# Second MLP's weight units: cast, low part and stores at other places in a pair of steps

## The chip, the cores and the metric

The kernel runs on one core of a Trainium2 chip. The metric is the device time of one execution in microseconds; of several runs the median is taken. Engines are named as the profile names them: PE (TensorE), DVE (VectorE), ACT (ScalarE), POOL (GpSimd) and SP (SyncE), whose queue, SPq, issues nearly all transfers.

## The reference

Three layers follow one another over 2304 tokens (4 batches of 576) of width 512:

```
attention, per batch and head (8 heads of 64):
    scores = (q @ k.T) / sqrt(64)
    out    = (scores * D) @ v          D[i, j] = gamma_h ** (i - j) for i >= j, else 0
first MLP:    h = max(x @ w_in, 0);   y = (h * h) @ w_out        512 -> 2048 -> 512
second MLP:   h = x @ w_in;  g = h * clip(h + 3, 0, 6) / 6;  y = g @ w_out
```

All inputs and the output are float32.

## The kernel before

**Precision.** PE multiplies in a shortened float32 (fp32r). Each operand is therefore held as a high part (its value cast) and a low part (the value less its high part), and a product is three matmuls: high by high, low by high, high by low.

**First stage.** The attention is computed as a recurrence over 18 chunks of 128 tokens and feeds the first MLP directly. The tokens of the first MLP go in five blocks of 512, 384, 512, 384 and 512 columns (`BLOCKS`, blocks 0 to 4), each in 16 steps over the 2048 inner columns: 80 steps, counted by `i` in the main loop. In step `i` the program writes, in this order: unit work of slot 0; `h_part` of step `i + 1` (12 matmuls at L514, then ACT's relu at L523, DVE's product at L525, ACT's high part of g at L527); unit work of slot 1; DVE's low part of g (L533); a piece of the attention for a later block (`retention`); and `a_part` of step `i` (12 matmuls at L551 that need g of this step). Each engine works its own list in the order written, and waits at an instruction until what it needs is there. PE's order in a step is therefore h of the next step, the piece of attention, a of this step.

**Retention.** In most even steps of blocks 1 to 3 a chunk has either its scores and states (L399, L410; DVE L418, L435, L437; then loads of the next chunk's k and q, L235, L236) or its values (L447, L457; ACT L468 and DVE L469 take the output into x; then loads of v, L243, and four small loads of qs, L383).

**Units.** The second MLP multiplies with seven products of combined blocks in place of eight, so its weights are combined once, in DRAM, while the first stage runs: 32 units, one begun every two steps from step 14 on. With `i - 14 = 2n + odd`, `unit_work` hands unit `n` and the units behind it to:

- `unit_load` (L596): two loads of raw words into `raw`, one buffer;
- `unit_scale` (L602, L603, ACT): scales the words;
- `unit_narrow` (L610, L611, DVE): joins them to float32 in a tile `seven`, of which there are two;
- `unit_combine` (four DVE operations, L618 to L621 or L623 to L626);
- `unit_cast` (L631, ACT): the high parts into `uhi`, tag "high", one buffer;
- `unit_low` (L636, DVE): the low parts, in place in `seven`;
- `unit_store` (L643 for the in-weights, L645 for the out-weights): 448 KB of high parts (`x` = 0) or low parts (`x` = 1) to DRAM.

A tile whose buffer was stored from is written again only when that store has landed. In step 72 (`half`) the loads of the second MLP's x (L691) are written behind the step's retention, and in the steps behind it DVE and ACT make x's operands (L695, L698, L702). Then the last units' work, the eviction of block 4 and the second MLP follow, in which PE runs L1025 and L1079.

Of the kernel before, what the change touches and what calls it, by code (L numbers as in the profile page):

```python
# [25 lines left out]
NF = DFF // P  # L26
# [58 lines left out]
def retention_moe_kernel(ctx: ExitStack, tc, qk, kv, w1, w2, cst, out):  # L85
# [144 lines left out]
    def load_qk(c):  # L230

        if c < NCHUNK:
            t = apool.tile([P, 2, NPAIR, P], F32, tag="q", name=f"q_{c}")
            k = apool.tile([P, DM], F32, tag="k", name=f"k_{c}")
            nc.sync.dma_start(k, kv[c, :, 0])  # L235
            nc.sync.dma_start(t, qk[c].rearrange("p x (n t) -> p x n t", n=NPAIR))  # L236
            ch[c] = [t[:, 0], t[:, 1], k]
# [147 lines left out]
    def scale_q(c):  # L385
        eng(c).tensor_tensor(qs[c], qs[c], since, ALU.mult)  # L386

    def scale_k(c):
        k3 = ch[c][2].rearrange("p (h d) -> p h d", h=H)
        eng(c).tensor_tensor(k3, k3, kd.unsqueeze(2).to_broadcast([P, H, D]), ALU.mult)  # L390

    def scores(c):
        q, kt, k, v = ch[c]
        _, straddle, ends = where(c)
        at = sums[c] = ps_at.tile([P, 2, 512], F32, tag="at", name=f"sc_{c}")
        for n in range(NPAIR):
            for e in range(2):
                for i in range(2):
                    nc.tensor.matmul(  # L399
                        at[hb(i), e, BT * n : BT * n + BT],  # L400
                        kt[hb(e), n, hb(i)],
                        q[hb(e), n, hb(i)],
                        start=True,
                        stop=True,
                    )

        for n in range(NPAIR):
            for i in range(1 if straddle else 0, 1 if ends else 2):
                for e in range(2):
                    nc.tensor.matmul(  # L410
                        at[hb(e), i, 256 + D * n : 256 + D * n + D],
                        k[hb(i), cols(n, e)],
                        v[hb(i), cols(n, e)],
                        start=True,
                        stop=True,
                    )
        t = probs[c] = apool.tile([P, 2, NPAIR * BT], F32, tag="p", name=f"p_{c}")
        nc.vector.tensor_tensor(t, at[:, :, :256], decay, ALU.mult)  # L418

    def age_state(c):  # L420
        new_state(c + 1)
        fresh, straddle, _ = where(c)
        if fresh or straddle:
            return
        m3, b3 = (t.rearrange("p (h d) -> p h d", h=H) for t in (middle(c), before(c)))
        nc.vector.tensor_tensor(m3, b3, gh[:BT].unsqueeze(2).to_broadcast([BT, H, D]), ALU.mult)

    def sum_states(c):
        fresh, straddle, ends = where(c)
        for i in range(1 if straddle else 0, 1 if ends else 2):  # L430
            for e in range(2):
                u = sums[c][hb(e), i, 256:].rearrange("p (n d) -> p n d", n=NPAIR)
                o = heads((before(c + 1) if i else middle(c)), e)
                if (fresh, straddle)[i]:
                    nc.vector.tensor_copy(o, u)  # L435
                else:
                    nc.vector.tensor_tensor(o, u, heads(middle(c), e), ALU.add)  # L437

    def values(c):
        v = ch[c][3]  # L440
        fresh, straddle, _ = where(c)
        at = os_[c] = ps_at.tile([P, 2, 512], F32, tag="at", name=f"o_{c}")
        read = [i for i in range(2) if not (fresh, straddle)[i]]
        for n in range(NPAIR):
            for i in range(2):
                for e in range(2):
                    nc.tensor.matmul(  # L447
                        at[hb(e), i, BT * n : BT * n + BT],
                        v[hb(i), cols(n, e)],
                        probs[c][hb(i), e, BT * n : BT * n + BT],  # L450
                        start=n == 0,
                        stop=n == NPAIR - 1 and i not in read,
                    )
        for n in range(NPAIR):
            for i in read:
                for e in range(2):
                    nc.tensor.matmul(  # L457
                        at[hb(e), i, BT * n : BT * n + BT],
                        rec[c][hb(i), cols(n, e)],
                        qs[c][hb(i), block(n, e)],  # L460
                        start=False,
                        stop=n == NPAIR - 1,
                    )

    def into_x(c, xt, off):
        x4 = xt[:, :, :, off : off + P].rearrange("p x n (i t) -> p x n i t", i=2)
        o = os_[c][:, :, :256].rearrange("p i (n t) -> p n i t", n=NPAIR)
        nc.scalar.activation(x4[:, 0], o, AF.Copy)  # L468
        nc.vector.tensor_tensor(x4[:, 1], o, x4[:, 0].bitcast(F32), ALU.subtract)  # L469
# [5 lines left out]
    def retention(i):  # L475
        for c, s in enumerate(SCORES, n0):
            if i == s - 1:
                scale_k(c)
                age_state(c)
            elif i == s:  # L480
                scores(c)
                if c < 7:
                    scale_q(c)
                else:
                    sum_states(c)
                load_qk(c + 1)
            elif i == s + 1:
                if c < 7:
                    sum_states(c)
                else:  # L490
                    scale_q(c)
            elif i == s + 2:
                blk = next(b for b in range(nblk) if start[b + 1] > c * P)
                values(c)
                into_x(c, xs[0, blk], c * P - start[blk])
                load_v(c + 1)
# [150 lines left out]
    def unit_work(i, slot):  # L647

        n, odd = divmod(i, 2)

        def on(lag, fn, *a):
            if 0 <= n - lag < 4 * NJ:
                fn(n - lag, *a)

        if slot == 0 and not odd:
            on(1, unit_narrow)
            on(0, unit_load)
            on(2, unit_store, 0)
        elif slot == 0:
            on(2, unit_low)  # L660
            on(2, unit_store, 1)
        elif not odd:
            on(1, unit_combine)
        else:
            on(0, unit_scale)
            on(1, unit_cast)


    x_ops = {}
# [156 lines left out]
    def first_between(f):  # L826
        if f + 2 < NF:
            cast_w(0, f + 2, (0,))
            low_w(0, f + 2, (0,))

    for i, (ph, blk, f) in enumerate(steps):
        if blk == 0:
            if 0 < f:
                low_w(0, f, (1,), nc.vector)
            if f == 0:
                first_sum(n0 - 1)
            if f + 3 < NF:
                scale_w(0, f + 3, (0,))
            if f + 2 < NF:
                scale_w(0, f + 2, (1,))  # L840
                narrow_w(0, f + 2, (0,))
            if f + 1 < NF:
                narrow_w(0, f + 1, (1,))
        unit_work(i - NF + 2, 0)
        if i + 1 < len(steps):
            h_part(*steps[i + 1], lambda: first_between(f) if blk == 0 else None)
            if blk == 0 and f + 1 < NF:
                cast_w(0, f + 1, (1,))
        if blk == 0:
            if f + 4 < NF:  # L850
                load_w(0, f + 4)
        if f < NF - 1:
            unit_work(i - NF + 2, 1)
        if i + 1 < len(steps) and blk:
            g_low(*steps[i + 1])
        if blk + 1 < nblk:
            if f == 0:
                new_x(0, blk + 1)
        retention(i)
        if blk == 0:  # L860
            g_low(*steps[i + 1])
        if i == half:

            right.close()
            p1a = xpre = pool(ctx, "p1a", 1, side="right")
            x_tiles(p1a)
            x_first = x_stages(0)
            for st in x_first:
                do(st[0])
        if half < i <= half + RING - 1:  # L870
            ring_load(i - half - 1)
        if i > half:
            k = i - half
            if k < len(x_first[0]):
                for st in x_first:
                    do(st[k])
        a_part(ph, blk, f)
        if f == NF - 1 and blk + 1 < nblk:
            evict(blk)
            unit_work(i - NF + 2, 1)  # L880
# [1 line left out]

    unit_work(len(steps) - NF + 1, 1)
    for v in range(len(steps) - NF + 2, len(steps) - NF + 4):
        unit_work(v, 0)
        unit_work(v, 1)
    left.close()
    p1c = pool(ctx, "p1c", 1, side="left")
    held = [
# [242 lines left out]
```

## Time and profile before

| | |
|---|---|
| median of 3 runs | 826.24 us (826.21 to 828.54) |
| the profiled execution | 825.94 us, its span 824.1 us |
| PE busy | 805.2 us (98%) |
| DVE busy | 597.0 us (72%) |
| ACT busy | 391.9 us (48%) |
| POOL busy | 164.1 us (20%) |
| SP's DMA queue | 188.40 MB, 72.6% of 16 engines |
| mean granted clock of PE | 0.998 of 2.4 GHz |
| mean of one, ACT | relu L523 0.55 us, g L527 0.59, x L468 0.58, cast L631 0.94 |
| mean of one, DVE | product L525 0.63 us, g's low part L533 0.68, unit's low part L636 1.08 |
| the four x loads of step 72 (L691) | issued from 429.79 on, the last at 432.09 |
| a pair of steps of block 2 (512 columns), with retention | 12.2 us between L551 groups at 211.80 and 224.00 |

Busy time tells how much an engine worked, not whether anyone waited for it. A wait in the profile is put down to the work that came last before the engine went on. Times of the trace are counted from the span's start. The first stage takes about 468 us of the span, the second MLP six stretches of 58.2 us on PE, and the tail 6.5 us.

### The profile page before, as it was taken

To read this page: it belongs to the slowest core of one execution; us is meant where nothing else is said; L and a number is where in the kernel's file an instruction comes from. 1 tells how busy PE (TensorE), PEld (TensorE's weight loads), DVE (VectorE), ACT (ScalarE), POOL (GpSimd) and SP (SyncE) were. 2 spreads that over 40 slices of the span, in tenths; PEclk is the share of its full clock that TensorE was granted. 3 is DMA by queue.
4 is the path that set the end of the run, shared out by engine and by line. 5 is a ranking of instruction groups with operands and counts; after the bars stand their busy time and mean duration, and the time that the engine had idled before them with its cause. 6 is when DMAs were issued, how large, how long until landed. Compare 5 with 4: busy or idle time off the path is not lost.

```text
span 824.1 us, 15603 instructions
## 1 busy us (share of the span) xinstructions
PE 805.2 (98%) x5876; PEld 744.6 (90%) x5876; DVE 597.0 (72%) x1098; ACT 391.9 (48%) x724; POOL 164.1 (20%) x146
## 2 busy tenths in 40 slices
PE   8999999988999999989999999999999999999996
PEld 7788889987888889989888899999999999999996
DVE  5888887566765576667546877988677987678764
ACT  1887744333433444334445433566234655334552
POOL 3312230111011001100000055600155400355300
PEclk9999999999999999999999999999999999999999
DMA  8876625666666466657447797889987979987785
GB/s 330 303 250 216 219 68 167 186 191 187 216 196 206 144 199 195 200 167 219 148 136 252 225 351 251 294 308 277 273 273 241 344 260 289 274 261 262 259 258 109
DMA packets 181899, 189.59 MB, mean 230 GB/s; under 512 B 60608, under 2 KB 135488, under 8 KB 181824
## 3 DMA queue, kind: packets, MB, share of 16 engines
q1 hardware_dynamic: 180224, 188.40, 72.6%
q8 instruction: 46, 0.75, 0.4%
q10 hardware_dynamic: 1600, 0.20, 0.2%
q14 instruction: 29, 0.24, 0.1%
HBM read 149.76 MB, written 38.80 MB: 229 GB/s over the span
## 4 chain that ended last, share of the span: by engine, by line
PE 83%; DVE 7%; DMA 5%; ACT 2%; issue 2%; SPq 1%; POOL 0%; DVEq 0%
PE z L1025 21%; PE z L1079 21%; PE acc L551 19%; PE h L514 18%; DMA w_in_hl<-seven 3%; DMA w_out_hl<-seven 1%; DMA kv<-kv_dram 1%; DVE r L525 1%; DVE seven L636 1%; DVE seven L611 1%; PE o L447 1%; SPq L383 1%; PE sc L399 1%; DVE state L437 1%; PE o L457 1%
## 5 line engine op out<-in xcount | busy, mean ns | idle before, releaser
L551 PE MATMUL acc<-g,w 128*128 128x512 f32 (+1 forms) x960 | 215.0, 372 | 4.9 <-ACT g L527 4.4
L514 PE MATMUL h<-x,w 128*128 128x512 f32 (+2 forms) x972 | 210.9, 365 | 1.6 <-ACT w L165 0.9
L551 PEld LDWEIGHTS acc<-g,w 128*128 128x128 f32 x960 | 172.9, 188 | 31.6 <-ACT g L527 6.8
L514 PEld LDWEIGHTS h<-x,w 128*128 128x128 f32 x972 | 175.8, 188 | 24.4 <-ACT w L165 1.6
L1025 PE MATMUL z<-xop,ring 128*128 128x384 f32 x1008 | 175.2, 334 | 0.0
L1079 PE MATMUL z<-spl,ring 128*128 128x384 f32 x1008 | 175.2, 334 | 0.0
L1025 PEld LDWEIGHTS z<-xop,ring 128*128 128x128 f32 x1008 | 174.8, 188 | 0.1
L1079 PEld LDWEIGHTS z<-spl,ring 128*128 128x128 f32 x1008 | 174.8, 188 | 0.0
L947 POOL TENSOR_TENSOR aop<-aop,aop 128x384 f32<-128x384 f32 x96 | 107.7, 1133 | 301.5 <-DVE aop L944 180.6
L961 DVE TENSOR_TENSOR spl<-aop,spl 128x384 fp32r<-128x384 f32 x168 | 97.8, 608 | 22.3 <-ACT spl L957 21.4
L957 ACT ACTIVATE spl<-aop 128x384 fp32r<-128x384 f32 x168 | 85.9, 523 | 55.3 <-PE z L1079 52.3
L527 ACT ACTIVATE g<-r 128x512 fp32r<-128x512 f32 (+1 forms) x80 | 47.1, 589 | 112.4 <-DVE r L525 112.4
L941 ACT ACTIVATE aop<-held,con 128x384 f32<-128x384 f32 x72 | 44.4, 617 | 108.1 <-DVE held L907 107.5
L523 ACT ACTIVATE r<-h 128x512 f32<-128x512 f32 (+1 forms) x80 | 44.2, 552 | 108.3 <-PE h L514 107.0
L525 DVE TENSOR_TENSOR r<-r,h 128x512 f32<-128x512 f32 (+1 forms) x80 | 50.5, 631 | 54.5 <-ACT r L523 53.9
L907 DVE TENSOR_TENSOR held<-z,held 128x384 f32<-128x384 f32 x120 | 66.5, 554 | 26.7 <-PE z L1025 24.4
L533 DVE TENSOR_TENSOR g<-r,g 128x512 fp32r<-128x512 f32 (+1 forms) x80 | 54.5, 681 | 22.2 <-ACT g L527 22.0
L944 DVE SCALAR_TENSOR_TENSOR aop<-aop,held 128x384 f32<-128x384 f32 x72 | 49.8, 692 | 17.8 <-ACT aop L941 16.1
L610 DVE TENSOR_SCALAR seven<-uraw 128x512 int32<-128x512 int32 x32 | 13.8, 432 | 40.1 <-DMA w_in_hl<-seven 18.3
L386 POOL TENSOR_TENSOR qs<-qs,con 128x512 f32<-128x512 f32 x11 | 14.7, 1336 | 121.1 <-DMA qs<-qk_dram 84.6
L172 POOL TENSOR_TENSOR w<-wt,w 128x512 fp32r<-128x512 f32 x17 | 22.4, 1322 | 72.6 <-ACT w L165 58.8
L636 DVE TENSOR_TENSOR seven<-seven,uhi 128x896 fp32r<-128x896 f32 x32 | 34.7, 1084 | 0.3
(88 smaller groups left out, 598.9 us busy)
## 6 DMA issues: line engine op xcount, KB each, us to landing
ring<-w_out_hl SPq DMA_DIRECT2D x84, 512.0 KB, 4.8
ring<-w_in_hl SPq DMA_DIRECT2D x72, 512.0 KB, 4.8
raw<-w_dram SPq DMA_DIRECT2D x32, 512.0 KB, 7.5
uraw<-w_dram SPq DMA_DIRECT2D x64, 256.0 KB, 3.2
q<-qk_dram SPq DMA_DIRECT2D x17, 512.0 KB, 5.4
w_in_hl<-uhi SPq DMA_DIRECT2D x16, 448.0 KB, 4.5
w_in_hl<-seven SPq DMA_DIRECT2D x16, 448.0 KB, 3.7
w_out_hl<-uhi SPq DMA_DIRECT2D x16, 448.0 KB, 4.3
```

Source lines behind the costliest of these rows:

```text
L514: nc.tensor.matmul(hp[:, ts], w[:, wi, c * P : (c + 1) * P], x[:, xi, c, ts], start=k == 0, stop=k == 3 * NC - 1,)
L525: nc.vector.tensor_tensor(r, r, hp[:, :nb], ALU.mult)
L527: nc.scalar.activation(g[:, 0, :nb], r, AF.Copy)
L533: nc.vector.tensor_tensor(g[:, 1, :nb], r, g[:, 0, :nb].bitcast(F32), ALU.subtract)
L551: nc.tensor.matmul(acc[d][:, :nb], wt, g[:, gi, :nb], start=first, stop=stop)
L907: fn(*a)
L944: stt(f32(q, j), f32(q, j), 6.0, h, ALU.min, ALU.mult)
L947: nc.gpsimd.tensor_tensor(f32(o, j), f32(a, j), f32(b, j), op)
L957: act(t[:, 0, :], f32(q, k), AF.Copy)
L961: tt(t[:, 1, :], f32(q, k), t[:, 0, :].bitcast(F32), ALU.subtract)
L1025: nc.tensor.matmul(bank[q], w[:, wi, u * P : (u + 1) * P], x[:, u, xi, :], start=k == 0 and q not in (2, 4, 3), stop=k == 5, skip_group_ch ...
L1079: nc.tensor.matmul(z[A_BANKS[q][n]][:, :HALF], w[:, k % 2, wi, P * n : P * (n + 1)], sp[:, g, :], start=k == 0 and m == 0 and q not in (2, ...
```

## The change

Three calls move. Let unit m be the one narrowed and combined in an even step. Its cast stood in the odd step behind, in slot 1; it now stands in the even step itself, behind the combination. Its low part stood in the odd step after the next, in slot 0; it now stands in the first odd step behind the combination. Its high parts were stored in the next even step, in slot 0, and its low parts behind the low part; both stores now stand in a third slot, behind the step's retention and so behind the loads of the chunk: the high parts at the end of the even step, the low parts at the end of the odd one.

```diff
@@ unit_work
         if slot == 0 and not odd:
             on(1, unit_narrow)
             on(0, unit_load)
-            on(2, unit_store, 0)
         elif slot == 0:
-            on(2, unit_low)
-            on(2, unit_store, 1)
+            on(1, unit_low)
+        elif slot == 2:
+            on(1, unit_store, odd)
         elif not odd:
             on(1, unit_combine)
+            on(1, unit_cast)
         else:
             on(0, unit_scale)
-            on(1, unit_cast)
...
@@ the main loop
         retention(i)
+        unit_work(i - NF + 2, 2)
         if blk == 0:
             g_low(*steps[i + 1])
         if i == half:
...
     for v in range(len(steps) - NF + 2, len(steps) - NF + 4):
-        unit_work(v, 0)
-        unit_work(v, 1)
+        for slot in range(3):
+            unit_work(v, slot)
```

The order on the engines, where the text below speaks of it. SP in block 1, one pair of steps and the beginning of the next, from the load of unit 5 on; the number behind `uraw`, `uhi` and `seven` is the unit's. Before:

```order
L596 DMA uraw_5_1977<-w2_dram 128x2x256 x2
L643 DMA w_in_hl1_105<-uhi_3_1958 896x1x128
L243 DMA v_10_2031<-kv_dram 128x512
L383 DMA qs_10_2033<-qk_dram 64x4x64 x4
L643 DMA w_in_hl1_105<-seven_3_1851 896x1x128
L596 DMA uraw_6_2093<-w2_dram 128x2x256 x2
```

And now:

```order
L596 DMA uraw_5_1980<-w2_dram 128x2x256 x2
L243 DMA v_10_2035<-kv_dram 128x512
L383 DMA qs_10_2037<-qk_dram 64x4x64 x4
L643 DMA w_in_hl2_106<-uhi_4_2005 896x1x128
L643 DMA w_in_hl2_106<-seven_4_1977 896x1x128
L596 DMA uraw_6_2096<-w2_dram 128x2x256 x2
```

The pair now stores unit 4 where it stored unit 3, and the high parts go behind v and qs.

ACT in the same pair of steps. Before:

```order
L523 ACTIVATE r_0_1_9_1994<-h_0_1_9_1981 128x384
L527 ACTIVATE g_0_1_9_1997<-r_0_1_9_1994 128x384
L468 ACTIVATE x_0_2_1520<-o_9_2004 128x4x128
L523 ACTIVATE r_0_1_10_2065<-h_0_1_10_2052 128x384
L527 ACTIVATE g_0_1_10_2068<-r_0_1_10_2065 128x384
L602 ACTIVATE uraw_5_1977<-uraw_5_1977 128x512
L603 ACTIVATE uraw_5_1977<-uraw_5_1977 128x512
L631 ACTIVATE uhi_4_2072<-seven_4_1974 128x896
```

And now:

```order
L523 ACTIVATE r_0_1_9_1996<-h_0_1_9_1983 128x384
L527 ACTIVATE g_0_1_9_1999<-r_0_1_9_1996 128x384
L631 ACTIVATE uhi_4_2005<-seven_4_1977 128x896
L468 ACTIVATE x_0_2_1522<-o_9_2008 128x4x128
L523 ACTIVATE r_0_1_10_2069<-h_0_1_10_2056 128x384
L527 ACTIVATE g_0_1_10_2072<-r_0_1_10_2069 128x384
L602 ACTIVATE uraw_5_1980<-uraw_5_1980 128x512
L603 ACTIVATE uraw_5_1980<-uraw_5_1980 128x512
```

The cast of unit 4 went from the end of the odd step to the even step, ahead of the chunk's output and of the next relu. On DVE the rows keep their kinds and places; in this pair L636 reads `seven_4` where it read `seven_3`.

SP at step 72, where the loads of x stand. Before:

```order
L596 DMA uraw_29_4623<-w2_dram 128x2x256 x2
L645 DMA w_out_hl_112<-uhi_27_4605 128x7x128
L691 DMA xtop_0_0_4663<-x1_103 128x768
L691 DMA xlow_0_0_4664<-x1_103 128x768
L691 DMA xtop_0_1_4668<-x1_103 128x768
L691 DMA xlow_0_1_4669<-x1_103 128x768
L645 DMA w_out_hl_112<-seven_27_4541 128x7x128
```

And now:

```order
L596 DMA uraw_29_4626<-w2_dram 128x2x256 x2
L645 DMA w_out_hl_112<-uhi_28_4651 128x7x128
L691 DMA xtop_0_0_4668<-x1_103 128x768
L691 DMA xlow_0_0_4669<-x1_103 128x768
L691 DMA xtop_0_1_4673<-x1_103 128x768
L691 DMA xlow_0_1_4674<-x1_103 128x768
L645 DMA w_out_hl_112<-seven_28_4623 128x7x128
```

The rows stand in the same order, but the store ahead of the x loads is that of unit 28, which is cast in this same step, where it was that of unit 27, cast in step 71.

## Rows read from the trace of the kernel before

**Rows 1.** Waits of PE: waiting line and releaser, us in total, times, longest.

```profile
PE acc L551 <- ACT g L527: 4.4, 5, 1.1
PE sc L410 <- issue: 2.3, 3, 1.4
```

**Rows 2.** Timeline of PE, blocks 1 and 3: start us, us, what.

```profile
128.10 2.35 PE L551 MATMUL acc<-g,w 128*128 128x384 f32 x12
...
189.19 2.35 PE L551 MATMUL acc<-g,w 128*128 128x384 f32 x12
...
207.85 2.92 PE L514 MATMUL h<-x,w 128*128 128x512 f32 x12
...
306.88 2.35 PE L551 MATMUL acc<-g,w 128*128 128x384 f32 x12
...
316.50 2.35 PE L551 MATMUL acc<-g,w 128*128 128x384 f32 x12
...
367.98 2.35 PE L551 MATMUL acc<-g,w 128*128 128x384 f32 x12
...
383.36 2.92 PE L514 MATMUL h<-x,w 128*128 128x512 f32 x12
```

**Rows 3.** Waits of DVE for stores of low parts.

```profile
DVE seven L610 <- DMA w_in_hl<-seven: 18.3, 6, 4.7
...
DVE seven L610 <- DMA w_out_hl<-seven: 8.7, 4, 4.4
```

**Rows 4.** Timeline of DVE, ACT and SP's queue, three narrowings of block 1.

```profile
149.11 0.43 DVE L610 TENSOR_SCALAR seven<-uraw 128x512 int32<-128x512 int32 x1 [4.70 <-DMA w_in_hl<-seven]
...
150.28 0.55 DVE L525 TENSOR_TENSOR r<-r,h 128x384 f32<-128x384 f32 x1
...
151.60 0.29 DVE L621 TENSOR_TENSOR seven<-seven 128x128 f32<-128x128 f32 x1
...
152.66 2.98 SPq L383 DMA_DIRECT2D qs<-qk_dram  x4
152.87 1.08 DVE L636 TENSOR_TENSOR seven<-seven,uhi 128x896 fp32r<-128x896 f32 x1
...
155.73 0.56 SPq L643 DMA_DIRECT2D w_in_hl<-seven  x1
...
159.21 0.64 DVE L610 TENSOR_SCALAR seven<-uraw 128x512 int32<-128x512 int32 x1 [3.64 <-DMA w_in_hl<-seven]
...
166.22 0.52 SPq L643 DMA_DIRECT2D w_in_hl<-seven  x1
...
168.34 0.94 ACT L631 ACTIVATE uhi<-seven 128x896 fp32r<-128x896 f32 x1
...
170.10 0.43 DVE L610 TENSOR_SCALAR seven<-uraw 128x512 int32<-128x512 int32 x1 [1.52 <-DMA w_in_hl<-seven]
```

**Rows 5.** Block 1: stretch, its us, busy us of PE, PEld, DVE, ACT, POOL.

```profile
128.00:207.00 79.00, 74.11 (x732) 69.93 (x725) 50.20 (x103) 30.10 (x55) 8.35 (x7) 1.00 0.61 181
```

**Rows 6.** The tile uhi: its 32 stores, from issue to landing.

```profile
DMA to landing us min/median/max: 3.6/4.4/6.2
```

**Rows 7.** Timeline around the x loads of step 72 and the last step.

```profile
429.79 0.51 SPq L691 DMA_DIRECT2D xtop<-x  x1
...
431.92 0.29 DVE L626 TENSOR_TENSOR seven<-seven 128x128 f32<-128x128 f32 x1
...
439.56 0.56 DVE L695 TENSOR_TENSOR xtop<-xlow,xtop 128x384 f32<-128x384 f32 x1
...
446.79 0.69 DVE L525 TENSOR_TENSOR r<-r,h 128x512 f32<-128x512 f32 x1 [2.10 <-ACT r L523]
...
462.28 5.79 PE L551 MATMUL acc<-g,w 128*128 128x512 f32 x24
...
464.77 0.68 DVE L533 TENSOR_TENSOR g<-r,g 128x512 fp32r<-128x512 f32 x1
```

**Rows 8.** Transfers between 425 and 445 us: KB each, median us to landing.

```profile
xlow<-x SPq DMA_DIRECT2D x2, 384.0 KB, 5.5
```

## The prediction

> **What bounds the kernel now.** I read the page's busy table first: TensorE (PE) is busy 805.2 of 824.1 us. So only PE's idle time and its slow restarts can be won, and the first question is where they are. The waits of PE name two that lie in the middle of the program [rows 1]: the second matmul of the first MLP (L551) waits five times, 4.4 us, for ACT's copy of g, and the state matmul (L410) three times, 2.3 us, for nothing the profile shows. PE's timeline tells where: all eight are in blocks 1 and 3, the blocks of 384 columns. The second MLP has none.
>
> Idle time undercounts, since each stop also breaks the overlap of matmuls. So I measure the loss by periods [rows 2]. In block 3 an undisturbed pair of steps, from one L551 group behind retention matmuls to the next but one, takes 316.50 - 306.88 = 9.62 us. Six such pairs would be 57.72. Block 3 takes 367.98 - 306.88 = 61.10 for them, block 1 189.19 - 128.10 = 61.09: 3.38 and 3.37 lost. The rest of block 1, up to the first group of block 2's second h, takes 207.85 - 189.19 = 18.66; the same stretch of block 3, which shows no stop, 383.36 - 367.98 = 15.38: 3.28 lost. Together **10.0 us**.
>
> What ends those waits? ACT's g waits for DVE's product r, and DVE's longest foreign wait is L610, the narrowing of a unit, for the store of a low part: 18.3 + 8.7 us in ten waits [rows 3]. One round of it is in [rows 4]. Unit 2 is narrowed at 149.11, unit 3 at 159.21, unit 4 at 170.10: periods of 10.10 and 10.89 us, where PE's pair takes 9.62. The round closes on itself. Between two narrowings DVE does the product, the combination, g's low part, a chunk's retention work and then the low part of the unit before; its store goes out behind that at 166.22, and the next narrowing needs that buffer ("seven" has two), so it starts when the store has landed, at 170.10, 3.88 us later. In the other kind of pair the low part ends at 153.95, but SP is issuing the four loads of qs (152.66 to 155.64), so the store goes at 155.73 and lands at 159.21. DVE falls back 0.5 to 1.3 us in a pair until its lead is gone; then PE waits. In a 512-column block the same pair of steps is longer than this round, and PE stops nowhere there.
>
> By the Trainium skill (DMA: Bandwidth & Descriptors, "Anatomy of one DMA") a transfer costs about 2.0 us plus its bytes over 436 GB/s, fitted for the other kind of queue; for 448 KB that is an estimate of 3.1 us. With it the two rounds would be 9.7 and 10.1 us, and the loss over 14 pairs about 3.5 us instead of 10. The landings here took 3.5 to 3.9 us, so the rows decide.
>
> **The change part by part.** No instruction is added or taken away, and every byte is moved as before. DVE's order is the same slot by slot: L636 stands where it stood, but works on the unit just combined instead of the one before. What moves is three things.
>
> *The low part and its store come two steps earlier for their unit.* The buffer that a narrowing takes was then stored at the end of the odd step two steps and more back. In narrow pairs that is about 9.6 us plus the rest of that step, against a landing of 3.5 to 3.9: the wait of L610 goes, 27 us on DVE, and with it the round. What is late next? The narrowing then waits for the scaling of its raw words on ACT, unchanged. DVE itself is busy 50.20 of 79.00 us in block 1 [rows 5], 6.1 of the 9.62 of a pair on average. So PE becomes the bound in blocks 1 and 3. SP's load of the next unit stands behind the narrowing, and v and k behind that, so L410's 2.3 us go too. Gain: 10.0 us at most; nothing at least, if another wait takes its place (rivals). I take all of it, since every successor I can find has microseconds to spare.
>
> *The high part's cast (L631) moves from the odd to the even step, directly behind the combination.* It costs 0.94 us on ACT [rows 4]. Counted from the end of an h on PE: relu 0.5, then product to end of combination 151.89 - 150.28 = 1.6, so the cast runs from 2.1 to 3.1. The next relu is due after retention, L551 and the next h, at about 5.5. Between them ACT has only the copy of the chunk's output (0.6): 1.8 us spare, so it costs nothing. The low part behind it on DVE can start at 3.1, where DVE is still busy with the chunk in most pairs.
>
> *The high part's store goes to the end of the even step, behind the chunk's loads.* "high" has one buffer, so the next cast waits for this store. With the qs loads in front (0.65 for v, 3.0 for qs, from 1.2 on) it goes out at 4.9 and lands, at the median of 4.4 [rows 6], at 9.3; the next cast is due at 9.6 + 2.1 = 11.7. Spare: 2.4 us, and 1.8 more on ACT before PE sees it. The largest landing of 32, 6.2, uses 1.8 of it.
>
> *One place gets worse.* In step 72 the four loads of x for the second MLP stand behind this store, which now waits for the cast of unit 28 [rows 7]. They went out from 429.79 on. The combination ends at 431.92 + 0.29 = 432.2, the cast at 433.2, the store's issue at 433.6, so they go from 433.7, 3.9 us later. The last, issued at 432.09, then goes at 436.0 and lands 5.5 later [rows 8], at 441.5; DVE's last difference used it at 439.56. DVE is up to 2.0 us late there. Of that a wait of 2.10 us at 446.79 can take up all, if ACT, which now has the cast in front of x's copies, does not pass on its own delay. What is left meets the last step, where PE begins the final a at 462.28 + 2.72 = 465.0 and its third matmul wants g's low part, which ends at 464.77 + 0.68 = 465.45: no spare at all. So the cost is 0 to 2.0 us. Nearest to the row with the 2.10 us I take 0.5.
>
> In the tail a cast, a low part and two stores come off the end of the first MLP; PE does not wait there, so zero. The second MLP is PE without a gap, and stays.
>
> Sum against the profiled run: 825.94 - 10.0 + 0.5 = 816.4. The median of the runs shown is 0.3 above that run, the highest 2.6; I predict **816.5**.
>
> **The rivals.** *A, the round is replaced by a shorter one.* If the high part's store behind qs lands late in the pairs with qs loads only, or raw words come late, half of the loss stays: 826 - 5 = 821. Against it speak the spare microseconds above. Chance 0.08.
>
> *B, no change.* The stops would have another cause, for instance DMA engines that are too slow for what a narrow pair moves, or the state matmul's late operand; L551 and L410 wait as before and the time is 825 to 827. For it: L410's three waits have no releaser in the profile. Against: the waits of L610 end with a landing, and the DMA engines are busy 0.61 of block 1 [rows 5]. Chance 0.04. That the change does not do what it says is excluded by the order above.
>
> *C, slower.* The one-buffer "high" becomes the round: cast, store behind the chunk's loads, landing, next cast, with relu behind the cast on ACT and PE behind relu. It holds PE once a landing takes more than 4.4 + 2.4 + 1.8 = 8.6 us. From there each microsecond costs 14 us over the 14 pairs of blocks 1 and 3. At 9.6 us it would be 816 + 14 = 830. No landing of these stores exceeded 6.2, but none of them was issued behind qs. Chance 0.04. The Trainium skill (same page and section) says that a wait for a semaphore is spent on the issuing sequencer and not in the DMA engines; that is the rule that speaks against stores at a step's end, and the trace agrees, with the store held back at 155.73 by SP's own issues.
>
> **How the numbers follow.** The forecast has 0.84: 815.4 without any loss at step 72 (815.9 in the profiled run, less half a microsecond for the scatter between runs) to 818 with all of it. A has 0.08 (818 to 823.5), B 0.04, C 0.04. The range that leaves out no more than 2 in 10 goes from 815.0 to 819.5. A measurement of this kernel can tell about 0.3%, 2.5 us, from no change: faster than 823.7 has 0.84 + 0.08 = 0.92, within 0.04, slower 0.04.
>
> **What would show it.** L610's waits for stores of "seven" disappear from DVE's list; L551's for ACT's g and L410's without a releaser go from PE's; six pairs of block 1 and of block 3 take 57.7 us each; the second MLP begins near 458.5 instead of 467.91. The x loads go out some 4 us later within step 72, and a short wait of DVE at L695 appears. The prediction is wrong if L631 waits for a store of uhi, if L551 still stops in blocks 1 and 3, or if the last step's L551 loses more than 2 us.

## The result and the profile after

The changed kernel takes 816.12 us (median of 4 runs, 815.93 to 817.65) against 826.23 us before (825.55 to 828.54): a ratio of 0.9877, 95% interval 0.9854 to 0.9899. The forecast was 816.5, the range 815.0 to 819.5. The profiled execution took 816.24 us with a span of 814.4, where the sum in the prediction gave 816.4.

The list of PE's waits after the change, the counterpart of [rows 1]. Its columns are the same: waiting line, releaser, us in total, times, longest.

```profile
PE h L514 <- ACT w L165: 1.0, 1, 1.0
...
PE h L514 <- POOL w L172: 0.5, 1, 0.5
...
PE acc L551 <- DVE g L533: 0.3, 1, 0.3
```

L551's five waits for ACT's g and L410's three without a releaser are gone. What is left lies before block 1, except the last line shown, which is the final step of the first MLP. DVE's list after has no line of L610 at all, where [rows 3] had 27 us (40.1 with L610's waits for other releasers). What it has in their place:

```profile
DVE x L469 <- ACT x L468: 16.6, 14, 1.7
...
DVE seven L636 <- ACT uhi L631: 4.4, 9, 0.6
...
DVE xtop L695 <- DMA xlow<-x: 1.4, 2, 0.9
...
DVE xdif L695 <- DMA xtop<-x: 0.8, 2, 0.6
```

The first two come from the cast's new place: on ACT it stands ahead of the chunk's output, and DVE's low part waits for it. The last two are the x loads of step 72. Only these last two reach PE, as block 4 and the experiment on step 72 show below.

PE's timeline after, the counterpart of [rows 2]:

```profile
128.06 2.35 PE L551 MATMUL acc<-g,w 128*128 128x384 f32 x12
...
185.76 2.35 PE L551 MATMUL acc<-g,w 128*128 128x384 f32 x12
...
300.17 2.35 PE L551 MATMUL acc<-g,w 128*128 128x384 f32 x12
...
357.88 2.35 PE L551 MATMUL acc<-g,w 128*128 128x384 f32 x12
...
452.18 3.73 PE L551 MATMUL acc<-g,w 128*128 128x512 f32 x14
456.17 2.56 PE L551 MATMUL acc<-g,w 128*128 128x512 f32 x10 [0.26 <-DVE g L533]
458.56 11.63 PE L1026 MATMUL z<-xop,ring 128*128 128x384 f32 x66
```

Six pairs take 57.70 us in block 1 and 57.71 in block 3, the 57.72 of undisturbed work. The second MLP of the kernel before began here:

```profile
467.91 12.32 PE L1025 MATMUL z<-xop,ring 128*128 128x384 f32 x70
```

From 452.18 to the second MLP at 458.56 it is 6.38 us, where the kernel before took 467.91 - 462.28 = 5.63: 0.75 us lost in the last step.

The same reading by blocks, for this kernel and the kernels of the experiments below: from the first h (L514) of a block to the first h of the next, and of block 4 to the first matmul of the second MLP. In the kernel before these begin at 119.79, 201.00, 298.72, 378.49 and 467.91 us, in the changed one at 119.74, 196.28, 292.01, 368.39 and 458.56. The last a of block 1 falls into block 2's stretch, and with it block 1's last stop.

| us | block 1 | block 2 | block 3 | block 4 |
|---|---|---|---|---|
| before | 81.21 | 97.72 | 79.77 | 89.42 |
| after | 76.54 | 95.73 | 76.38 | 90.17 |
| e1_low_store_other_source | 76.53 | 95.74 | 76.38 | 89.42 |
| e2_before_low_twice | 91.48 | 95.87 | 88.25 | 93.33 |
| e3_after_low_twice | 76.54 | 95.73 | 76.38 | 90.40 |
| e4_after_high_twice | 76.53 | 95.73 | 76.38 | 92.28 |
| e5_x_loads_first | 76.54 | 95.74 | 76.38 | 89.42 |
| e6_stores_ahead_of_chunk | 76.54 | 95.73 | 76.38 | 90.18 |
| e7_cast_in_odd_step | 78.57 | 98.01 | 80.58 | 95.33 |
| e8_odd_cast_low_behind_narrowing | 76.54 | 95.73 | 76.39 | 90.27 |

Blocks 1 to 3 gave back 258.70 - 248.65 = 10.05 us; block 4 took 0.75. The span fell by 9.7; the other 0.4 lie behind the start of the second MLP, 814.4 - 458.56 = 355.8 against 356.2 us.

### The profile page after: what moved, and what is told of

It reads as the page before. It is cut to its first block, busy times and chain, and to the rows that moved or that the text cites. A ratio compares the mean times of both kernels' runs of the same rounds, so it can differ in the third digit from the quotient of the medians.

```text
span 814.4 us, 15623 instructions
## 1 busy us (share of the span) xinstructions
PE 802.7 (99%) x5876; PEld 744.5 (91%) x5876; DVE 600.1 (74%) x1098; ACT 397.3 (49%) x724; POOL 166.4 (20%) x146
## 4 chain that ended last, share of the span: by engine, by line
PE 91%; DVE 3%; DMA 2%; ACT 2%; issue 1%; SPq 0%; POOL 0%; DVEq 0%; ACTq 0%
PE acc L551 23%; PE h L514 22%; PE z L1026 21%; PE z L1080 21%; PE o L447 1%; PE sc L399 1%; DMA kv<-kv_dram 1%; PE o L457 1%; PE sc L410 1%; DMA xlow<-x 1%; DVE r L525 0%; DVE xop L702 0%; ACT raw L138 0%; ACT raw L139 0%; DVE p L273 0%
## 5 line engine op out<-in xcount | busy, mean ns | idle before, releaser
L551 PE MATMUL acc<-g,w 128*128 128x512 f32 (+1 forms) x960 | 214.2, 371 | 0.4 <-DVE g L533 0.3
L514 PE MATMUL h<-x,w 128*128 128x512 f32 (+2 forms) x972 | 210.8, 365 | 1.6 <-ACT w L165 1.0
L514 PEld LDWEIGHTS h<-x,w 128*128 128x128 f32 x972 | 175.8, 188 | 24.4 <-ACT w L165 1.6
L551 PEld LDWEIGHTS acc<-g,w 128*128 128x128 f32 x960 | 173.1, 188 | 25.1 <-DVE g L533 0.7
L525 DVE TENSOR_TENSOR r<-r,h 128x512 f32<-128x512 f32 (+1 forms) x80 | 50.6, 633 | 62.2 <-ACT r L523 61.6
L631 ACT ACTIVATE uhi<-seven 128x896 fp32r<-128x896 f32 x32 | 30.5, 954 | 16.7 <-DVE seven L621 8.4
L636 DVE TENSOR_TENSOR seven<-seven,uhi 128x896 fp32r<-128x896 f32 x32 | 35.0, 1095 | 4.7 <-ACT uhi L631 4.4
```

The lines of the kernel that those rows point to most:

```text
L514: nc.tensor.matmul(hp[:, ts], w[:, wi, c * P : (c + 1) * P], x[:, xi, c, ts], start=k == 0, stop=k == 3 * NC - 1,)
L525: nc.vector.tensor_tensor(r, r, hp[:, :nb], ALU.mult)
L551: nc.tensor.matmul(acc[d][:, :nb], wt, g[:, gi, :nb], start=first, stop=stop)
```

## The experiments

Each ratio is to runs of the kernel before that were timed beside the kernel in question; their medians were 826.8 to 828.1 us.

**Is the wait for the landing the whole loss?** In the kernel before, the store of low parts reads another tile of the same size, so that nothing waits for it. The low parts of the second MLP's weights are then not stored: this kernel leaves them out and does not compute the reference.

```diff
-        part = units[n][1 - x].bitcast(F32)
+        if x:
+            w = wts[0, NJ, 0].rearrange("p a n -> p (a n)")[:, : 7 * P]
+            part = w.rearrange("p (s n) -> p s n", s=7).bitcast(F32)
+        else:
+            part = units[n][1].bitcast(F32)
```

> The kernel before, except that the stores of low parts read a weight tile of the first MLP that nobody overwrites, of the same size, to the same place and at the same point of the queue; the low parts of the second MLP's weights are so not stored (the output is wrong by it). Bytes and issues stay; only the wait of the narrowing for the landing goes. Theory (the round narrowing, low part, store, landing, narrowing is the whole loss): the 10 us come back without any other move, and the x loads of step 72 stay where they were, so 815.4 to 816.3. Rival (the DMA engines or late chunk loads are the cause): bytes unchanged, so 823 to 826.

Measured: 815.62 us, ratio 0.9858 (0.9834 to 0.9882). All ten microseconds come back in the order of before, with the same bytes on the same queue, and block 4 loses nothing. So neither the DMA engines' rate nor the place of the chunk's loads was the cause: rival B falls.

**Does the loss grow with the landing?** A second store of each low part, to spare tensors, once in the kernel before and once in the changed one.

```diff
+    spare = [dpool.tile([P, 7, P], F32, tag=f"spare{k}", name=f"spare{k}") for k in range(2)]
...
+        if x == 1:
+            nc.sync.dma_start(spare[n % 2], part)
```

> The kernel before with every low part stored a second time, to a spare tensor in DRAM, directly behind the first store. Theory: the landing that closes the round comes later by the second store's issue (0.5) and its 448 KB (some 1.2 us at the 390 GB/s seen around step 72), so the rounds of 10.1 and 10.9 us become about 11.5 and 12.3; 14 narrow pairs lose 1.4 us each more, the 512-column pairs of 12.2 us hardly: 840 to 850. Rival (only the bytes count): the same, but then the changed kernel with the same second store loses as much.

> The changed kernel with the same second store of every low part. Theory: the buffer is needed two steps later, so 1.4 us more of landing are hidden: 816 to 817.5. Rival (bytes): it loses what the kernel before loses by it, 830 to 840.

Measured: 850.09 us for the kernel before with it, ratio 1.0275 (1.0248 to 1.0302), and 817.15 for the changed kernel with it, 0.9879 (0.9850 to 0.9907). DVE's and SP's timeline of the first:

```profile
173.74 0.43 DVE L611 TENSOR_SCALAR seven<-uraw 128x512 int32<-128x512 int32 x1 [2.14 <-DMA spare<-seven]
...
177.50 1.08 DVE L637 TENSOR_TENSOR seven<-seven,uhi 128x896 fp32r<-128x896 f32 x1
...
181.50 0.56 SPq L644 DMA_DIRECT2D w_in_hl<-seven  x1
182.11 0.65 SPq L648 DMA_DIRECT2D spare<-seven  x1
...
186.18 0.43 DVE L611 TENSOR_SCALAR seven<-uraw 128x512 int32<-128x512 int32 x1 [5.26 <-DMA spare<-seven]
```

Lines are shifted by one here: L611 is the narrowing, L637 the low part. The rounds are 12.4 us (173.74 to 186.18) and, to 199.77, 13.6, where [rows 4] had 10.1 and 10.9; 11.5 and 12.3 were expected. Blocks 1 to 3 lose 275.60 - 258.70 = 16.9 us more than before, in the narrow blocks; the 512-column block 2, whose pair takes 12.2 us, is at 95.87 against the 95.73 of the changed kernel. Two losses were not foreseen: 3.9 us in block 4, whose last L551 waits 1.77 us for ACT's g, and 2.8 us behind the start of the second MLP. They take the time just over the range. In the changed kernel the same 14 MB more cost nothing in blocks 1 to 3. That is the greater distance between store and narrowing at work, and it rules out the bytes a second time.

**How near is the one buffer of high parts to its limit?** The changed kernel, with each high part stored twice (`x == 0` in the line above).

> The changed kernel with every high part stored a second time, to a spare tensor, directly behind the first store at the even step's end. The next cast waits for both. Theory: 2.4 us are spare before the next cast and 1.8 more before PE, and the second store takes about 1.7 of them: 816 to 818, with L631 perhaps waiting for a store in a few pairs, and step 72's x loads about 0.5 us later. Rival (the one buffer of the high parts is at the edge): each microsecond beyond costs up to 14 us, 820 to 835.

Measured: 818.29 us, ratio 0.9891 (0.9866 to 0.9916), just above what was expected. Blocks 1 to 3 do not change by more than 0.01 us, and no wait of the cast (here L632) for a store appears: the spare microseconds were there, and rival C did not come. They were nearly used up, though. The tightest pair:

```profile
313.80 0.55 SPq L648 DMA_DIRECT2D spare<-uhi  x1
...
320.78 0.95 ACT L632 ACTIVATE uhi<-seven 128x896 fp32r<-128x896 f32 x1 [0.58 <-DVE seven L627]
```

This second store took 6.7 us to land, so it was there 0.3 us before the next cast. Block 4 takes the 2.1 us (another 1.0 us of the profiled run lies behind the start of the second MLP). The second store stands in front of the x loads too, and DVE's waits for them, L698 in this kernel and L695 in the changed one, grow from 2.2 to 4.3 us:

```profile
DVE xdif L698 <- DMA xtop<-x: 2.5, 2, 2.0
DVE xtop L698 <- DMA xlow<-x: 1.8, 2, 1.1
```

Block 4 is 0.75 us longer than before with 2.2 us of these waits and 2.86 us longer with 4.3. By these two kernels PE loses what goes beyond some 1.4 us.

**Where do the 0.75 us in block 4 come from?** In step 72 the store goes behind the x loads.

```diff
         retention(i)
-        unit_work(i - NF + 2, 2)
+        if i != half:
+            unit_work(i - NF + 2, 2)
...
             for st in x_first:
                 do(st[0])
+            unit_work(i - NF + 2, 2)
```

> The changed kernel, except that in step 72 the store of high parts stands behind the four x loads in place of ahead of them. Theory (the store, waiting for the cast, holds the x loads, DVE waits 2.2 us at L695 for them, and the last step of the first MLP loses 0.75 us on PE): the loss goes, DVE's waits at L695 go, the second MLP begins 0.75 us earlier, about 815.4. Rival (the loss in the last step comes from the cast's place ahead of x's copies on ACT): 816.1 and the stop in the last step stays.

Measured: 815.48 us, ratio 0.9857 (0.9835 to 0.9878). The interval overlaps that of the changed kernel, so the times alone do not tell the two apart; the traces do. Of this kernel and, behind it, of the changed one, the timeline of SP, ACT and DVE:

```profile
417.60 0.89 SPq L596 DMA_DIRECT2D uraw<-w_dram  x2
418.58 0.42 SPq L691 DMA_DIRECT2D xtop<-x  x1
...
422.58 0.37 SPq L645 DMA_DIRECT2D w_out_hl<-uhi  x1
...
428.86 0.56 DVE L695 TENSOR_TENSOR xtop<-xlow,xtop 128x384 f32<-128x384 f32 x1
```

```profile
418.20 0.89 SPq L596 DMA_DIRECT2D uraw<-w_dram  x2
...
422.19 0.96 ACT L631 ACTIVATE uhi<-seven 128x896 fp32r<-128x896 f32 x1 [0.47 <-DVE seven L626]
...
423.17 0.37 SPq L645 DMA_DIRECT2D w_out_hl<-uhi  x1
...
423.63 0.51 SPq L691 DMA_DIRECT2D xtop<-x  x1
...
431.75 0.56 DVE L695 TENSOR_TENSOR xtop<-xlow,xtop 128x384 f32<-128x384 f32 x1 [0.46 <-DMA xlow<-x]
```

From the unit's load to the first x load it is 0.98 us with the loads first and 5.43 in the changed kernel, because SP stands at the store until the cast has ended (422.19 + 0.96 = 423.15; the store goes at 423.17). With the loads first L695 waits for nothing, and block 4 takes 89.42 us, as before the change. The cast's place on ACT, the rival, is the same in both. Of the changed versions that compute the reference its traced block 4 is the shortest, by 0.75 us.

**Does it matter that the stores stand behind the chunk's loads?** Each store directly behind its cast or low part.

```diff
         elif slot == 0:
             on(1, unit_low)
+            on(1, unit_store, 1)
         elif slot == 2:
-            on(1, unit_store, odd)
+            pass
         elif not odd:
             on(1, unit_combine)
             on(1, unit_cast)
+            on(1, unit_store, 0)
```

> The changed kernel with each store directly behind its cast or low part, so ahead of the chunk's loads. Theory (only the distance between a low part's store and the narrowing counts): SP is held until the cast ends, some 3.1 us behind the end of h, so k, q, v and qs go out about 2 us later, which has 6 us and more to spare: 816 to 816.6. Rival (the place behind the chunk's loads is part of the gain): waits of L410 or L447 come back on PE, 818 to 824.

Measured: 816.27 us, ratio 0.9875 (0.9848 to 0.9901), every block within 0.01 us of the changed kernel. The store's place behind the chunk's loads adds nothing to the other two parts: v goes out at 150.36 here, behind a store that waited for its cast, in place of 147.41, and PE does not wait for it.

**Is the early cast needed?** The cast back in the odd step, the low part and both stores at that step's end.

```diff
-        elif slot == 0:
-            on(1, unit_low)
         elif slot == 2:
-            on(1, unit_store, odd)
+            if odd:
+                on(1, unit_low)
+                on(1, unit_store, 0)
+                on(1, unit_store, 1)
         elif not odd:
             on(1, unit_combine)
-            on(1, unit_cast)
-        else:
+        elif slot == 1:
             on(0, unit_scale)
+            on(1, unit_cast)
```

In the last step of a block slot 2 stands behind slot 1 in this kernel (the code for it is not shown).

> The changed kernel with the cast where it was, in the odd step behind the scaling, and the low part and both stores at the end of that odd step. The low part's store then lies two steps ahead of the narrowing that takes the buffer, as in the changed kernel. DVE waits for the cast in each pair, about 1.7 us, and the narrowing stands behind that. Theory: that fits into DVE's idle time, and x's loads are not held: 815.4 to 816.5. Rival (the early cast is needed, since a low part in the odd step's end delays the next narrowing): DVE falls behind in blocks 1 and 3, 819 to 826.

Measured: 829.89 us, ratio 1.0032 (1.0015 to 1.0049), a little slower than the kernel before. My expectation was wrong. I had counted the time that DVE loses at the cast, 1.7 us, and not asked whether it closes a round. A line of DVE's list of waits, one passage of the timeline, and the last L551 of block 4:

```profile
DVE seven L636 <- ACT uhi L631: 50.0, 29, 4.6
```

```profile
169.27 1.66 SPq L596 DMA_DIRECT2D uraw<-w_dram  x2
175.41 0.65 ACT L602 ACTIVATE uraw<-uraw 128x512 f32<-128x512 f32 x1 [2.57 <-DMA uraw<-w_dram]
...
176.51 0.94 ACT L631 ACTIVATE uhi<-seven 128x896 fp32r<-128x896 f32 x1
177.48 1.09 DVE L636 TENSOR_TENSOR seven<-seven,uhi 128x896 fp32r<-128x896 f32 x1 [3.32 <-ACT uhi L631]
178.49 0.42 DVE L610 TENSOR_SCALAR seven<-uraw 128x512 int32<-128x512 int32 x1
```

```profile
466.23 5.63 PE L551 MATMUL acc<-g,w 128*128 128x512 f32 x12 [2.65 <-ACT g L527]
```

The load of raw words waits for the narrowing before, since there is one buffer for them; the scaling waits for its landing; the cast stands behind the scaling on ACT; the low part waits for the cast; and the next narrowing now stands behind the low part. That is a new round of 10.3 us on average (seven narrowings of block 1 from 136.87 to 198.73), again longer than 9.62. Block 4 loses 5.9 us against before, most of it at its last L551, which waits 2.65 us and then takes 5.63 in place of 2.88; the waits for the cast go on in the steps that make x's operands, but that they are the cause there is not shown.

**Is that the reason, or is an odd cast bad in itself?** The same cast, but the low part and its store behind the next narrowing and load. The cut below is against the kernel just shown.

```diff
         if slot == 0 and not odd:
             on(1, unit_narrow)
             on(0, unit_load)
+            on(2, unit_low)
+            on(2, unit_store, 1)
         elif slot == 2:
             if odd:
-                on(1, unit_low)
                 on(1, unit_store, 0)
-                on(1, unit_store, 1)
```

> The kernel with the cast in the odd step, as in e7_cast_in_odd_step, but the low part and its store stand behind the next narrowing and the next unit's load, at the head of the even step, and the store of high parts at the end of the odd step. Theory (in e7 the narrowing stood behind the low part, that behind the cast, that behind the scaling, and that behind the load of raw words, which waits for the narrowing before: a round of 10.3 us through the one buffer of raw words): the round is cut, the low part's store still goes out a step and more ahead of the narrowing that takes the buffer, so blocks 1 and 3 run without stops: 815.4 to 817. Rival (a cast in the odd step is itself too late or in ACT's way there): stops of L551 stay in blocks 1 and 3, 820 to 830.

Measured: 816.21 us, ratio 0.9862 (0.9843 to 0.9881), with blocks 1 to 3 at their undisturbed length. The low part is here only one step earlier than before the change, and the cast where it was. So neither the cast's early place nor the full two steps are what brings the gain. In this kernel it is enough that no chain with a landing in it, from one narrowing to the next, is longer than PE's pair. Block 4 is 0.85 us longer than before here too: in its last step DVE's low part, 1.08 us, stands ahead of the product, and L551 waits for g.

## Why the prediction was right

**What bounds.** The loss of 10.0 us by periods was right to 0.05: blocks 1 to 3 gave back 10.05. Adding up PE's waits would have given 6.7 [rows 1]; most of the rest was time in which PE counts as busy, which fell by 2.5 us, from 805.2 to 802.7. That the landing closes the round is now shown from both sides, by taking the wait away (e1_low_store_other_source) and by making the landing longer (e2_before_low_twice).

**The low part two steps earlier.** Right, with no successor: L610 has no wait in the list, and DVE is idle at L525 for ACT's relu instead, 61.6 us against 53.9. Of the two steps one would have done, as the last experiment shows.

**The cast behind the combination.** Right that it costs nothing. The first estimate of where it starts, 2.1 us behind the end of h, was near: 2.25 us in most narrow pairs (up to 2.7), 2.5 in the 512-column blocks, and 3.3 to 4.6 in the last three, behind step 72. It starts when the combination ends, after ACT has stood idle for 0.4 to 0.6 us. Its price on DVE, L469 and L636 waiting 21.0 us in all (against 5.1 for L469 before), was not in the text, and is covered by idle time.

**The store of high parts.** Right. One pair with qs and the one behind it, ACT's and SP's timeline of the changed kernel:

```profile
147.98 3.64 SPq L383 DMA_DIRECT2D qs<-qk_dram  x4
148.51 0.95 ACT L631 ACTIVATE uhi<-seven 128x896 fp32r<-128x896 f32 x1 [0.58 <-DVE seven L621]
...
151.72 0.56 SPq L643 DMA_DIRECT2D w_in_hl<-uhi  x1
...
158.13 0.95 ACT L631 ACTIVATE uhi<-seven 128x896 fp32r<-128x896 f32 x1 [0.58 <-DVE seven L621]
```

The store goes out behind qs and has 6.4 us until the next cast. Landings of these stores were 3.0 to 6.4 us with a median of 3.4; I had taken 4.4 from [rows 6]. No cast waited for one. The prediction's doubt was about the pairs with qs, but there they landed after 3.3 to 4.0 us. In the narrow pairs that load k and q they took up to 6.2 us, and the tightest of all, issued at 140.77, landed 1.5 us before the cast at 148.51.

**Step 72.** The mechanism was right and the size near. Counted from the first h of block 4, the x loads go 3.9 us later, as computed, and DVE's last difference (431.75 now, 439.56 in [rows 7]) is 2.3 us late, where 2.0 was forecast. PE's loss of 0.75 us is inside 0 to 2.0 and above the 0.5 taken. I let the wait at 446.79, 2.10 us long, take up more of it than it did; 1.05 us of it were left:

```profile
438.33 0.69 DVE L525 TENSOR_TENSOR r<-r,h 128x512 f32<-128x512 f32 x1 [1.05 <-ACT r L523]
```

This product is still 1.64 us late. In e5_x_loads_first the loss goes with the order of two entries in one queue.

**The total.** 816.24 in the profiled run against a sum of 816.4: the 0.25 us too little for step 72 and the 0.35 us that the second MLP and the tail ran shorter, which no step foresaw and no run explains, nearly cancel. That much of the agreement is luck.

**The rivals.** A and B did not come. C's price could not be shown, since even twice the store made no cast wait. The Trainium skill (DMA: Bandwidth & Descriptors, "Anatomy of one DMA") says that a wait for a semaphore is spent on the sequencer that issues the DMA. Step 72 agrees: SP stood at the store, and the x loads behind it went out 3.9 us late. The row named for it in the prediction, the store at 155.73, shows only that SP issues in order; that store's low part had ended at 153.95. The estimate of 3.1 us for a landing, worked out from the same section's fit for the other kind of queue, was below the 3.8 us median of the low parts' stores after the change. By the prediction's own working it would have made the gain about a third of what it was (14 pairs at the mean excess of its two rounds, 0.3 us, are nearer 4 us than the 3.5 written there).

## What to carry to other kernels

When an engine waits for a landing in a loop, follow the chain once round, from one use of the buffer to the next, and compare its length with the period of the engine that should bound; the loss is the excess, pair by pair, once the lead is used up. In these runs, moving work further was worth nothing more once the chain was shorter than the period, and a move that looked free closed another chain (e7_cast_in_odd_step). Behind a store that waits for a fresh result, look at what else is queued: in this kernel four loads in one step out of eighty were the whole price.

## What the runs showed of the hardware

PE's granted clock fell to half, 1.2 in place of 2.4 GHz, behind some stops, and stayed there for several microseconds, so that a stop cost more than its length. In e2_before_low_twice PE stood still for 3.44 us, and the 12 matmuls behind that took 4.21 us; 2.24 to 2.43 is usual there. Windows of that kernel: stretch, its us, busy us of PE, PEld, DVE, ACT and POOL, granted clock, share and rate of DMA.

```profile
195.00:201.00 6.00, 3.65 (x21) 3.21 (x19) 1.65 (x4) 1.42 (x3) 0.14 (x1) 1.00 0.38 131
201.00:204.00 3.00, 1.90 (x6) 1.90 (x7) 2.93 (x9) 1.39 (x3) 0.00 (x0) 0.54 0.55 178
204.00:207.00 3.00, 3.00 (x11) 3.00 (x10) 1.63 (x3) 1.89 (x4) 0.00 (x0) 0.50 0.98 276
207.00:210.00 3.00, 3.00 (x16) 3.00 (x16) 0.00 (x0) 1.12 (x2) 0.80 (x1) 0.82 1.03 306
```

The longest stop of the kernel before in these blocks, 1.44 us, left the clock at 1.00. In e2_before_low_twice a wait of 2.08 us did so too. One of 1.77 us did not: from 378 to 381 us the granted clock was 0.62.

```profile
365.34 2.37 PE L551 MATMUL acc<-g,w 128*128 128x384 f32 x12 [2.08 <-ACT g L527]
...
377.73 3.41 PE L551 MATMUL acc<-g,w 128*128 128x384 f32 x12 [1.77 <-ACT g L527]
```

So the length of a stop alone does not tell which it will be. The expectation for that kernel had no term for the clock.
